# Two cached attention blocks on one core: fewer DMA transposes of P, x loaded in three parts, a shorter warm-up, the output written into its accumulator

## The chip, the cores and the metric

The kernel runs on one core of a Trainium2 chip. The metric is the device time of one execution in microseconds (us), lower is better; the time of a kernel is the median of its runs.

## The reference

Two independent problems, A and B, of the same shape; their results are put side by side along the last axis. All tensors are bfloat16.

```python
# x (16, 80, 576), k_cache and v_cache (16, 16, 512, 128), wq (576, 32*128), wo (32*128, 576)
q = (x @ wq).reshape(B, Sq, Hq, Dh).transpose(0, 2, 1, 3)
k = jnp.repeat(k_cache, 2, axis=1)
v = jnp.repeat(v_cache, 2, axis=1)
scores = jnp.einsum("bhqd,bhkd->bhqk", q, k) * (Dh ** -0.5)
p = softmax(scores, axis=-1)
o = jnp.einsum("bhqk,bhkd->bhqd", p, v)
return o.transpose(0, 2, 1, 3).reshape(B, Sq, Hq * Dh) @ wo
...
return jnp.concatenate([a, b], axis=-1)
```

Each of the 16 heads of K and V serves two query heads, so a K head meets 2 x 80 = 160 query rows.

## The kernel before

**Steps.** The work is cut into 128 steps U, 64 for each problem. A step takes one batch element and four K heads. The 160 query rows of a K head don't fit the 128 rows of a tile, so a step has five score tiles of 128 x 512: one for the first 128 rows of each of the four heads (L678), and one "remainder" tile that collects the last 32 rows of all four (L665).

**What a step does.** TensorE (PE) makes the scores in a PSUM bank. VectorE (DVE) takes the row maximum (L687), ScalarE (ACT) the exponential with its row sum into a slot of `p_sb` (L691), DVE the reciprocal of the sums (L697), GpSimd (POOL) multiplies the slot by it (L700). PE transposes P in blocks of 64 x 64 (L733), and ACT or DVE evict the transposes into `pT` (L751 and L752 for the four main tiles, L757 and L758 for the remainder). PE multiplies `pT` by V (L781), the result goes to `oT` (L795).

**The remainder by DMA.** `rtr` says whether the remainder of a step goes another way: for `RT0 <= U < RT1` and odd U (`RTM`), SyncE (SP) issues a DMA transpose from `p_sb` to `pT` (L740), and PE and the evictions leave the remainder out, so that a step has 32 transposes on PE in place of 40. RT0 is 71 and RT1 is 124 here, which are 27 steps.

**Around the steps.** The projection of q (L542 with a tail of 64 rows in L555, evicted in L568 and L569) runs some steps ahead. The output projection (L827) is done for half of the heads at a time: the first half goes to `acc` in float32 (L839), the second is added and stored (L856 adds, L862 stores). The sum is written to `osb`, which has NOSB = 2 slots, and the store reads it there, so an add waits for the store two before it.

**The start.** GpSimd makes ones and the identity. PE does NWARM matmuls on constants (L353). The first half of x of problem A (five blocks of 128 rows) is loaded in two parts of three and two blocks from SP's queue (L380) into memory that `acc` uses later; GpSimd copies the last 64 columns (L388), PE transposes (L401, L419), DVE evicts (L406, L423). K comes by DMA transpose (L631), V, wq and wo by plain DMA (L635, L507 and L511, L595), all from SP's queue.

**Order.** The order of all instructions on all engines is written out in the string ORDER: each letter takes the next operation of one stream, a mark before it chooses the second engine for an eviction, digits name the PSUM banks. An engine takes its own in that order and waits on semaphores that a pass over the reads and writes works out.

Of the kernel before, what the change touches and what calls it, by code (L numbers as in the profile page):

```python
# [27 lines left out]
NWARM = 8  # L28
# [3 lines left out]
RT0 = 71  # L32
# [19 lines left out]
XLD = ((-100.0, -85.0), (-5.0, -4.9))  # L52
# [11 lines left out]
LETTERS = "abcdefghijklmnopqrstuvwxyzABCDEFGHIJKLMNOPQ"  # L64
ORDER = """
pGMpk7JMJJJJPKl3Gl4JOl5m6OKOKPl3l4Od5KNKd3Kd6ad7d2d1eee'CDd0Dd3CDd5Cd6d7eeDm2d1Dd3CNd6Od2d4Meee'D'CCMd0a'Dd7'D
'Cg1'Ceqg6'Dg2'Cqh5nh7qd3ng0rg1d4nreoqd6C'Dg2d5oqeEnqg4wg7jd3C'DQanqd0wl5Enql6wenOg1wg2Cd5'Dqxng4l3qd0nOqni67O
nEg1Eym3wz'Bqh24w'ADl7ng6xrc0jc'Cqwg1joc5rjwnag2qcoEd6Nwq'ug3'vd4wOnl5qh07nOEri15nwroQg2xd3A'y'Bd0wEq'Cg1oxzi5
6qnwDc7cywnBg4d2'uqg1'Ac7Cc'znm5Ec6qwcH'vg3ENg4'uwHqd7njwDi56naqwh01'zA'yx'Dc3Bng5g7cq'Cc6'vcEqnc4wg2d3rnwcEud
5owqi67'vwrng0Ezb4'AwyD'Bqwog2g7xqg6bnq'Cg0nsd3qnc4g1qcjng2d5Ejqxnai67uwnqh04w'AEyzc1'Crwg6'Bcd3Dnwqg7d5'vqoi1  # L70
2Ernwc0znwcEAc6c'ywu'Bg1g7Cog0xc2qc'Dwg3qc4ncvd5'ujqng1jd6qani27vnEEqxh04'Bzwb3E'yr'AwD'Cg2org7wc6cqnc5wcuod0w
vg1nqd6xqg5nwi24Eqnwg7zbnBwq'Ag1jg5'syd4jqnag2Dd3'Cqni67qnh01EEAnwc5cy'zwr'Bc6g2'ucwEqoc7cwrc5'vcnwg0Dd6Coxg3q
d4'uwvg1nb7qqng0i25HqnHEg3w'ABbj'zyanwqg1'sd5xD'Cqg0nc7cqng2d4unqh36Ei17nrxErob0Eoxg2g3'Aqbw'Bywqng1c7qwd6'z's
Dcnwg0Cd2nwqi34Ewvnjg1zw'yg7'Aqjd5w'Dac3qng0cCd2nBc6'ucqh17vni34ErxEg6E'BAwc0c'z'yd4rwoc3uxocqc1g0w'Ccvng7qc5w
c'uqg3wnb6vwnqjg0d5jqnai17EE'Dwng3Bd2w'Azg0qwg7bDwnqd5'yqni13C'sh04'yz'ABc6'Dcrng1c3qg5ocb7qnCg0'uErjbw'vanqwd
3osxg1g2nqc7d4EEnqwci56wnh01zx'ABg2'Dc5w'yqg6'Cg4cqnb3EEu'vxnd2qjwg7rc5Lwd6qjocwjbnuawng0wi45qrb7'AyozCbEBwg1D
s'swc4cnqg2xc7'vg6qd3nEd4nwEqcg0wui15nxh27ywqb6zwrj'DbnIBj'Ag0Losd4Cc6qcg1'vc3rcng2Eqd5wa'ug0qnwi36nb1B'Aqog2c
3qg6nbq'znyg0g7'Dqcnc2d5ECw'vqc'sd4wni36x'uh01'AyECwg2'z'Bc3Eqcj'Dxg5nc6vLb4wqjjwErbIwoLg7wjcnqd3wnud0rni26Esw
g5y'Bc7xqd4'ACg6'zwncDc2jcqoc3ag0u'vd5qng1cqni27vnEh06EzwB'yg3'Ad1wq'Cd7'Dxrng2i45rwoqwc3'AcEyg0'Bwzc4D'Ccwg5n
# [861 lines left out]
```

## Time and profile before

| | |
|---|---|
| Runs | 718.01, 720.44, 720.60 us; median 720.44 |
| Profiled execution | 720.92 us; its span is 719.0 us |
| Clock of TensorE in the profile | 1.00 |
| PE, DVE, ACT, POOL busy | 712.0, 630.0, 637.5, 431.9 us |
| DMA moved | 164.23 MB, 228 GB/s over the span |

A span is the time from the first to the last instruction of the profiled execution. Rows of the timeline give the start, the length, the engine, the line of the kernel and the operation with its tiles; in brackets stands the idle time before it and what ended it. Matmuls overlap, so the length of one is not its price; the distance from start to start is.

### The profile page before, as it was taken

Reading aid. Unit: us, or ns where it says so; the run is one execution under the profiler, and the core shown is the slowest. Engines: PE = TensorE matmul, PEld = TensorE weight load, DVE = VectorE, ACT = ScalarE, POOL = GpSimd, SP = SyncE. Lnnn points to the kernel's source line nnn. Section 1 sums busy time; section 2 is a strip of 40 time slices with the busy share of each in tenths; the row PEclk is TensorE's granted clock in tenths of the full one; section 3 lists DMA queues with packets and bytes.
Section 4 is the critical chain, followed back from the end, with each engine's and each line's share of the span. In section 5 each row is a group of like instructions: output and inputs, shape, how many; then the busy total and the mean of one; then the engine's idle time right before and its main releaser. Section 6 shows DMA issues by size and latency. Waiting matters only on the chain.

```text
span 719.0 us, 25863 instructions
## 1 busy us (share of the span) xinstructions
PE 712.0 (99%) x10604; PEld 508.8 (71%) x10604; DVE 630.0 (88%) x1419; ACT 637.5 (89%) x1830; POOL 431.9 (60%) x650
## 2 busy tenths in 40 slices
PE   9999999999999999999999999999999999999998
PEld 5576777777777777777777776767677777777777
DVE  3999998899978998899998899878898889998995
ACT  1999998899988998799988999888999898998994
POOL 0467657566655765755774566645676466665783
PEclk9999999999999999999999999999999999999999
DMA  9999999999799998999999999999999999999970
GB/s 238 275 217 240 273 252 250 286 232 244 175 268 241 220 241 194 258 223 240 255 216 248 226 201 206 228 246 239 220 229 204 279 196 261 225 247 221 211 195 18
DMA packets 388853, 164.23 MB, mean 228 GB/s; under 512 B 293248, under 2 KB 385664, under 8 KB 388736
## 3 DMA queue, kind: packets, MB, share of 16 engines
q1 hardware_dynamic: 388736, 162.59, 100.2%
q8 instruction: 84, 1.38, 0.8%
q14 instruction: 33, 0.27, 0.2%
HBM read 87.65 MB, written 2.95 MB: 126 GB/s over the span
## 4 chain that ended last, share of the span: by engine, by line
PE 93%; DMA 2%; DVE 2%; ACT 1%; SPq 0%; issue 0%; ACTq 0%; DVEq 0%
PE ps L827 22%; PE ps L781 20%; PE ps L542 18%; PE ps L678 15%; PE ps L733 10%; PE ps L665 5%; PE ps L555 4%; DVE negmax L687 2%; DMA pT<-p_sb 1%; DMA wq_sb<-in_A_wq_dram 1%; DMA out_dram<-osb 1%; ACT p_sb L691 0%; ACT qT L568 0%; DVE xT L406 0%; DVE qT L569 0%
## 5 line engine op out<-in xcount | busy, mean ns | idle before, releaser
L700 POOL TENSOR_SCALAR p_sb<-p_sb,rinv 128x512 bf16<-128x512 bf16 x640 | 430.1, 692 | 271.4 <-DVE rinv L697 270.8
L691 ACT ACTIVATE p_sb<-ps,negmax 128x512 bf16<-128x512 f32 x640 | 442.7, 713 | 27.3 <-DVE negmax L687 23.5
L687 DVE TENSOR_REDUCE negmax<-ps 128x1 f32<-128x512 f32 x640 | 419.2, 682 | 35.0 <-PE ps L678 30.3
L781 PE MATMUL ps<-pT,v_sb 128*128 128x160 bf16 x2048 | 191.2, 233 | 1.1 <-ACT p_sb L691 0.8
L781 PEld LDWEIGHTS ps<-pT,v_sb 128*128 128x128 bf16 x2048 | 152.8, 98 | 42.6 <-ACT p_sb L691 4.1
L827 PE MATMUL ps<-wo_sb,oT 128*128 128x288 bf16 x1280 | 181.1, 286 | 0.0
L678 PE MATMUL ps<-kT,qT 128*128 128x512 bf16 x512 | 178.0, 380 | 1.2 <-ACT p_sb L691 0.8
L542 PE MATMUL ps<-xT,wq_sb 128*128 128x320 bf16 x1024 | 174.4, 299 | 0.2 <-DMA wq_sb<-in_A_wq_dram 0.2
L827 PEld LDWEIGHTS ps<-wo_sb,oT 128*128 128x128 bf16 x1280 | 122.0, 98 | 42.5 <-ACT p_sb L691 0.8
L691 ACT ACTIVATION_READ_ACCUMULATOR p_sb<-ps,negmax 128x1 f32 x640 | 146.0, 228 | 0.0
L542 PEld LDWEIGHTS ps<-xT,wq_sb 128*128 128x128 bf16 x1024 | 95.4, 98 | 45.0 <-ACT p_sb L691 2.4
L751 ACT COPY pT<-ps 128x512 f32<-128x512 f32 x157 | 92.4, 602 | 13.3 <-PE ps L733 12.8
L733 PEld LDWEIGHTS ps<-ident,p_sb 64*128 64x128 bf16 x4904 | 88.2, 95 | 7.3 <-issue 1.3
L733 PE MATMUL ps<-ident,p_sb 64*128 64x64 bf16 x4904 | 92.4, 190 | 0.3 <-issue 0.2
L752 DVE COPY pT<-ps 128x1024 bf16<-128x1024 bf16 x99 | 67.3, 684 | 11.4 <-PE ps L733 10.0
L568 ACT ACTIVATE qT<-ps 128x320 bf16<-128x320 f32 x133 | 59.0, 458 | 19.3 <-PE ps L555 15.5
L569 DVE TENSOR_SCALAR qT<-ps 128x320 bf16<-128x320 f32 x123 | 58.2, 482 | 10.7 <-PE ps L555 6.1
L795 DVE CAST oT<-ps 128x320 bf16<-128x320 f32 x122 | 58.4, 482 | 7.7 <-PE ps L781 7.4
L678 PEld LDWEIGHTS ps<-kT,qT 128*128 128x128 bf16 x512 | 48.0, 97 | 24.1 <-ACT p_sb L691 4.1
L795 ACT CAST oT<-ps 128x320 bf16<-128x320 f32 x134 | 58.9, 451 | 5.2 <-PE ps L781 4.9
L697 DVE RECIPROCAL rinv<-rowsum 128x3 f32<-128x3 f32 (+1 forms) x256 | 38.4, 160 | 1.8 <-ACT p_sb L691 1.7
L665 PE MATMUL ps<-kT,qT 128*32 128x512 bf16 x512 | 39.2, 384 | 0.0
(31 smaller groups left out, 175.5 us busy)
## 6 DMA issues: line engine op xcount, KB each, us to landing
v_sb<-in_A_v_cache_dram SPq DMA_DIRECT2D x64, 512.0 KB, 5.0
v_sb<-in_B_v_cache_dram SPq DMA_DIRECT2D x64, 512.0 KB, 5.2
wo_sb<-in_A_wo_dram SPq DMA_DIRECT2D x8, 576.0 KB, 5.8
wo_sb<-in_B_wo_dram SPq DMA_DIRECT2D x8, 576.0 KB, 5.8
wq_sb<-in_B_wq_dram SPq DMA_DIRECT2D x4, 1024.0 KB, 6.9
out_dram<-osb SPq DMA_DIRECT2D x40, 72.0 KB, 3.8
wq_sb<-in_A_wq_dram SPq DMA_DIRECT2D x8, 256.0 KB, 4.7
wq_sb<-in_A_wq_dram SPq DMA_DIRECT2D x2, 1024.0 KB, 8.4
```

The lines of the kernel that those rows point to most:

```text
L542: last = e.matmul(ps[:, vbq[h].phys, QO:QO + 320], lhsT=wq_sb[:, wsl, ck, hi * 128:(hi + 1) * 128], rhs=xT[:, half, ck, n0:n0 + 320], star ...
L665: last = e.matmul(ps[32 * g4:32 * g4 + 32, vb_.phys, :], lhsT=qT[:, qsl_, bl_, g4 * 160 + 128:g4 * 160 + 160], rhs=k_of(U_, g4), start=Tru ...
L678: return e.matmul(ps[:, vb.phys, :], lhsT=qT[:, qsl, bl, gl * 160:gl * 160 + 128], rhs=k_of(U, gl), start=True, stop=True)
L687: return e.tensor_reduce(negmax[:, si:si + 1], ps[:, vb.phys, :], axis=AX.X, op=AluOpType.max, negate=True)
L691: return e.activation(p_sb[:, psl, :], ps[:, vb.phys, :], AF.Exp, bias=negmax[:, si:si + 1], scale=1.0, accum_out=rowsum[:, ss, k:k + 1])
L700: return e.tensor_scalar(p_sb[:, psl, :], p_sb[:, psl, :], rinv[:, ss, k:k + 1], 1.0, op0=AluOpType.mult, op1=AluOpType.mult)
L733: last = e.matmul(dst, lhsT=p_sb[64 * h:64 * h + 64, psls[k_], j * 128:(j + 1) * 128], rhs=ident[64 * h:64 * h + 64, 64 * h:64 * h + 64], ...
L751: return e.copy(dst.bitcast(F32), ps[:, vtp[h].phys, :].rearrange("p (j n) -> p j n", j=4))
L752: return e.tensor_copy(dst, psb[:, vtp[h].phys, :].rearrange("p (j n) -> p j n", j=4))
L781: last = e.matmul(ps[:, vo.phys, off:off + 160], lhsT=v_sb[:, vs, gl, j * 128:(j + 1) * 128], rhs=pT[:, pts, j, :, 32 * gl:32 * gl + 32], ...
L795: return (e.copy if en == "act" else e.tensor_copy)(dst, src)
L827: last = e.matmul(ps[:, vb.phys, 0:DC], lhsT=oT[:, sp_ * (HH // 2) + i, rb * 128:(rb + 1) * 128], rhs=wo_sb[:, 2 * c3 + sp_, i, :], start= ...
```

## The change

- RT0 goes from 71 to 97: 14 steps send their remainder by DMA in place of 27. The other 13 transpose it on PE and evict it as the even steps do.
- The first half of x is loaded in three parts, of one, two and two blocks. The first is issued from ACT's queue, the others from SP's. Copies, transposes and evictions of the tail follow these parts.
- NWARM goes from 8 to 5.
- The last add writes its bfloat16 result over the first half of the float32 values that it reads in `acc`, and the store reads it there. `osb` is gone, and with it the wait of an add for an earlier store. An add of problem B into `acc` has the store of problem A from that place to wait for.
- ORDER is another one, with a stream more (the part of x on ACT's queue). On PE the groups of matmuls are partly in another order, and some evictions change between ACT and DVE. On GpSimd the copy of the first block of x stands ahead of the making of the identity.

```diff
-NWARM = 8
+NWARM = 5
...
-RT0 = 71
+RT0 = 97
...
-XLD = ((-100.0, -85.0), (-5.0, -4.9))
+XLD = ((-100.0, -99.9, -85.0), (-5.0, -4.9))
+XENG = (("act", "sp", "sp"), ("sp", "sp"))
...
-        osb = sb("osb", [128, NOSB, DC], BF16)
...
-        XP = ((0, 3), (3, 5))
+        XPS = (((0, 1), (1, 3), (3, 5)), ((0, 3), (3, 5)))
...
-            for part, (k0, k1) in enumerate(XP):
+            for part, (k0, k1) in enumerate(XPS[half]):
...
-                S.add("sp", XLD[half][part], em_ldx,
+                S.add(XENG[half][part], XLD[half][part], em_ldx,
...
-                xk = (XA + 4.0 * part if half == 0 else 5.0 * (16 - LQ) - XH) + 0.1 * part
+                xk = (XA + (0.0, 0.6, 4.0)[part] if half == 0 else 5.0 * (16 - LQ) - XH) + 0.1 * part
...
-                                return e.tensor_tensor(osb[:, slot, :], ps[:, vb.phys, 0:DC],
+                                return e.tensor_tensor(xs[:, rb, 2 * c3 * DC:(2 * c3 + 1) * DC], ps[:, vb.phys, 0:DC],
                                                        acc[:, rb, c3 * DC:(c3 + 1) * DC], AluOpType.add)
...
-                                return e.dma_start(dst, osb[:, slot, :])
+                                return e.dma_start(dst, xs[:, rb, 2 * c3 * DC:(2 * c3 + 1) * DC])
...
-                                  writes=[R(("osb", slot), (prob, half, n))], name="oeb%d.%d.%d" % (prob, half, n),
+                                  writes=[R(("acc", rb, c3), (prob, hh))], name="oeb%d.%d.%d" % (prob, half, n),
...
-                            S.add("sp", xe + 0.3, em_st, reads=[R(("osb", slot), (prob, half, n))],
+                            S.add("sp", xe + 0.3, em_st, reads=[R(("acc", rb, c3), (prob, hh))],
```

More of the change, by code (lines that the diff above doesn't have):

```diff
@@ L62 @@
 WOK = 6.0
-LETTERS = "abcdefghijklmnopqrstuvwxyzABCDEFGHIJKLMNOPQ"
+LETTERS = "abcdefghijklmnopqrstuvwxyzABCDEFGHIJKLMNOPQR"
 ORDER = """
[L66 to L79, printed above, removed]
@@ new lines @@
+g2ni14DEqowc0Ec'zAw'Bc3g7y'Dcwjqg1nc4Hg5wvncjqm2d3xH'COg7qEu'uad6ni24wnqxc1'Azg0ycEnwDh25q'Bwg6Cg7'vc4wrncg1qc
+3ocd0unqd2'vEg4qnwi36rnwb7q'ABog1g3EEg6q'zwbnqx'y'Dg5Cng4wd2sqnwc0d7jqnwcjqi13nxaEunwc6zcAg0'Dwh45'Bq'vg1rd3nE
+d6yoxri07qwoc4Cw'AcEBc5'ywg0'zncqg2wc7'ucDng1qd4'uEg6C'vc0wnqcjd3wq'vag7nxi25Eqnwg0Ad1'yw'z'BEDh26wnqg5b3rx'Cn
+rwc7og4qcc0oucg2vd7nqi06qnjg5zbjE'yq'Awj'CBg0awng4qd1ng6Dd2qni57snqh03'z'BEAwc4ncrc7wg5'ycE'uCc6wog4vcqwd1'uEb
+7rnwqoxg0c6qncwd3D'vg5Eng4wqi26wqHng0HbzxA'Bj'yqnag2g6d5D'sq'Cc4ncqg1d3nuh07qni24ErnxEb6roEoxg1g0qb'Aw'Byqwg2n
@@ new lines @@
+c7qd4w'z'sDcnwg1Cd6qnwi35Evwng0zg2w'y'Aqd7j'Dwjc1qng3acCd6nBc4'ucqh02vni15ErxEg4E'BAwc3c'z'yd5rwoc1uxocqc0g3w'
+Ccvng2qc7wc'uqg1wnb4vwnqg0d3qjni27jEE'Dwang1Bd6w'Azg0qwg7bDwnqd3'yqni12C'sh05'yz'ABc4'Dcrng1c3qg2ocb7qnCg0'uEr
+bw'vnqjwd3oasxg1g2nqc7d4EEnqwci56wnh01zx'ABg2'Dc5w'yqg6'Cg4cqnb3EEu'vxnd2qwg7rc5wd6jqocLwbnujwjng0awi45qrb7'Ay
+ozCbEBwg1Ds'swc4cnqg2xc7'vg6qd3nEd4nwEqcg0wui15nxh27ywqb6zwr'DbnBj'AIg0osd4jCc6Lqcg1'vc3rcng2Eqd5wa'ug0qnwi36n
+b1B'Aqog2c3qg6nbq'znyg0g7'Dqcnc2d5ECw'vqc'sd4wni36x'uh01'AyECwg2'z'Bc3Eqc'Dxg5nc6vb4wqjwELrbjwojg7wcInqd3Lwnud
@@ new lines @@
+0jrni26Eswg5y'Bc7xqd4'ACg6'zwncDc2jcqoc3ag0u'vd5qng1cqni27vnEh06EzwB'yg3'Ad1wq'Cd7'Dxrng2i45rwoqwc3'AcEyg0'Bwz
+c4D'Ccwg5nqc1cqd7nuc2'vcung0d3q'vg1og5Eqxi24nqwb6'ABwnzag0EDg2w'yg4nqbwqnd3Eq'Cxg1nc5qcwg0nd7swEq'uh26nwi45rnw
+rc1'Bjcd0'Ajvg5'zaog1qb4'yDoqc2cng7Euc6wncCg2wd5q'vg1qxni36EEnwbA'Bwq'yg2'zx'sg7qg6nc3wcEqnd4wDd1nuwi25jq'CwjE
+h07ay'BwzAc3ncwrg5'Dg2d6'Cqoc4rd1'vnqci03unEg5w'yb4oqwBng2xbq'z'CAnc7cg6'vg0qc3'Dd5jEqnwg1jcsd7njwqh26ni04r'uE
+Ec1w'Bzd3A'yowg4rcac0wCcoc2qwc'vg5Dng6xb1q'vxung2qd4qg0ni57qnEg6Awb'y'z'DBwng2Eqg5wc7g4sjd0nxqad1'Cwqncc3Eqcni
@@ new lines @@
+26uvh57A'Bd3'yE'zrnxc6cC'Dwg2Eg4orc1wb0qowqng5bwqnjwg2jnd7qwc'si45'uj'vh06'BzEDwg1'ynb5rxqd7wHng2bq'Aoc4Hscc1E
+'uwc'Cg0jd4'vwqng1ri35anqb2oA'y'zg0ng6qb'BEqw'Cc3ng1cwqg7'uc5xcnqd3vnd0Dnsi56h12'Bd4'yr'Ag7'CEg6wjqod5b3qwnMrn
+g1g7zbDEqwi06Esnwqb3owzAnwc1Eg2c'BxMqg0c7'uacwqnd6xb'D'ynwCg1'sg2qc4cd3qnEi05unwh14w'BzEg2'vrwc5'AcHqb7'ywoMHx
+'vg0ng1qbqng2td5'DqF'Cd7nEjri36jnc1Aocc2zg0'BycEqg4x'ujg6'Cc3q'vwcnc5qg1wcnDg2jd0wEq'uad7nwvi34Enqwh56wy'BECd1
+'z'Awrg0nm4wDd3qoxi27Onwc5'Acrwg0'yc4'BzcCog2c7qc'uc1qncg6vd5'uqng0d4Ejqnwai27DnxEvg6'Bg3wyb1q'Awqng0wd7q'Cg2'
@@ new lines @@
+zng6Eqg5wbnDwqng4xd3qni02tnqh16'BEjAwc5'zacnrc2wg0'DycEEg4'uCwc3'vqcoc7wg2qg5nxcqd1nwvd0'uqwi47nrb3EyowC'zg2w'
+Bd6q'Axg1jd7nqg4nbEqanEi25xtnwh13B'D'Ag4wzc0r'yc'Cwg2r'ug5c6owd0qocDd1qni37q'vc4B'zjncc6jug7'AcEyg2w'Dvjd4'CqF
+wnc3g0Fqd6ncqg1ni57EEuwnqh23x'yA'Bc0wc'z'Cg7Dc5'vwarcng0c4wEuog6cqxd5rnd2wqb1owvnqi37h04A'z'Dbr'ynjEwg2'Btg3g6
+oqc7wFcqjb1nEunwg0qbwqnxg2Etg7'Cc3qnwcd5rjnwd6Fai01b2A'B'vq'zg0'Dg1qd3nd6q'ync7Ccnb'uoh01ti57rc4'BFg2c'yIqob7z
+'vE'Dwg0b'CqnxAg6nwg4tg2d3qFb7EjEnEwqLg0qwbnaqwnc4tcwnc6ud5xg0wi47qwErc'Bb2xy'znAwg7bqwvng0g4qd6j'Doc7FEtwcLCc
@@ new lines @@
+5ncEwFqg1d3'ujqwni27vwd4znxDd5'yE'AwCh01M'Bwi36rg2A'zb7'Dqog5y'Bg3rbqoIc6CcnLtc1g0qMncc7aqg2'vd4nEuxcqd5nwg1'u
+c3qnwi06ng7zcq'Dg2g1'Ab5q'vnEywd3Eqng0wEg7qbnxqnd2wEt'Bg1wi05'CqjnxMh46A'ywnFc7zcFrw'Bc0Ld1E'DCwjocrg2wjd3'vqo
+ag5wui04nqwc7'yB'zg6'Acqc2'DcnCg0c3vg4ncqg1d5qqEEu'ung2d6ni03wnqh47w'z'yEB'Ad1wnrc0cwC'Dc3g2'vrxg6ocaqc5wcog0E
+qd4xnqb7wnuwm2ni36Ow'vg0'Bg5zbq'y'AEqnwg2c3t'DjcxEg0nqjg7wh46aq'unc5qcd3nCd2rni01voErxg7'Bb5qw'z'Aywg1nDc4qd0w
+ocg2wnuc7cq'Cg6d4'vqng1Ei37Eqwnjg2w'yzjbnAxq'Dg1'Bwg6Etg4nad3qwd5'Cqwni27qwnEh01Bw'znc6Dcw'Arg7d5'yxq'uc4'CcEo
@@ L133 @@
+3qnxA'Bg2wjh06qnjg1rc7ncqbou'vEc5tnxcc7rwi0234vowg1Bc'Ac5qg6'ucg4ynfg7Eqb3w'vqwng0Fqg1nbjEzwFqnFh26qwnai45rxc7
+'AEg0Bwcob4Etw'urnc7wqg2og5wg3qcb'vqnqc7nctc6ucng0vi1247nqjg6F'zEg5y'Awg2qFb1nFqxjnbqwFnEfBxg0ng6Eti34wqFh57'B
+wEjqc2njg1wcr'Ab4wunEqxc3og0cwqbnw'vni1256wtrFc3w'AcEBg0'zx'uc4c'yqog2wi1356vwqg7'Ac4Bc'ync5zg1qcng6c3vcnEuc5w
+c'ub0Ew'vqqxni3457wnbBw'y'zEAb7wtwc3Fci2456uc1'Ab'B'y'zcc3'vcc4ucb5tvFbb7tFbtF
 """
@@ L381, in em_ldx @@
                                        src.rearrange("(k p) d -> p k d", p=128))
-                S.add("sp", XLD[half][part], em_ldx,
+                S.add(XENG[half][part], XLD[half][part], em_ldx,
                       writes=[R(("xs", half * NRT + k_), 0) for k_ in range(k0, k1)], dsem="d_x%d%d" % (half, part),
-                      name="ldx%d.%d" % (half, part), stream="x")
+                      name="ldx%d.%d" % (half, part), stream="xa" if half == part == 0 else "x")
                 def em_xrp(e, half=half, k0=k0, k1=k1):
```

90 lines of the change are left out of this document (35 added, 55 removed).

## The prediction

> **What bounds the kernel now.** I read the page's first lines, then the busy time by stretches, then the timeline of the start, of the stretch that the new RT0 concerns, and of the end.
>
> ```profile
> span 719.0 us, 25863 instructions
> PE 712.0 (99%) x10604; PEld 508.8 (71%) x10604; DVE 630.0 (88%) x1419; ACT 637.5 (89%) x1830; POOL 431.9 (60%) x650
> ```
>
> ```profile
> 50.00:100.00 50.00, 50.00 (x766) 35.40 (x764) 48.73 (x112) 48.89 (x143) 33.54 (x51) 1.00 1.12 262
> ...
> 413.00:550.00 137.00, 135.33 (x2010) 96.26 (x2009) 120.90 (x267) 124.97 (x360) 86.59 (x129) 1.00 1.04 223
> 550.00:700.00 150.00, 149.64 (x2244) 108.88 (x2236) 134.03 (x297) 135.15 (x384) 95.52 (x144) 1.00 1.04 229
> ```
>
> In the stretches the columns are length, then busy time of PE, PEld, DVE, ACT and POOL, clock, DMA. TensorE (PE) is the bound nearly everywhere: 50.00 of 50 us between 50 and 100, 149.64 of 150 between 550 and 700. Only 413 to 550 us shows a loss, 1.67 us. That is where the odd steps from 71 on send their remainder by DMA; the DMA transposes go on after 550, where PE lacks only 0.36. So there is little idle time to win, and a change is worth the PE work that it adds, less the idle time that it takes away, plus what start and end do. All stretches show clock 1.00, so I take no change of clock later.
>
> **The remainder of P, added work.** RT0 rises from 71 to 97: the odd steps 71 to 95, 13 of them, return to PE. A step on the DMA path has 32 transposes on PE, another 40. The timeline of PE shows both kinds after each other; a group's cost is the distance from its start to the next group's start.
>
> ```profile
> 415.99 0.63 PE L733 MATMUL ps<-ident,p_sb 64*128 64x64 bf16 x32
> 416.55 0.73 PE L781 MATMUL ps<-pT,v_sb 128*128 128x160 bf16 x8
> 417.11 0.38 PE L678 MATMUL ps<-kT,qT 128*128 128x512 bf16 x1
> 417.33 0.71 PE L542 MATMUL ps<-xT,wq_sb 128*128 128x320 bf16 x4
> 417.87 0.44 PE L781 MATMUL ps<-pT,v_sb 128*128 128x160 bf16 x4
> 418.48 0.39 PE L678 MATMUL ps<-kT,qT 128*128 128x512 bf16 x1 [0.17 <-ACT p_sb L691]
> ...
> 419.68 0.38 PE L678 MATMUL ps<-kT,qT 128*128 128x512 bf16 x1
> 420.00 0.31 PE L555 MATMUL ps<-xT,wt 64*128 64x320 bf16 x2
> 420.14 0.75 PE L733 MATMUL ps<-ident,p_sb 64*128 64x64 bf16 x40
> 420.82 0.62 PE L665 MATMUL ps<-kT,qT 128*32 128x512 bf16 x8
> ```
>
> 32 transposes take 416.55 − 415.99 = 0.56 us, 40 take 420.82 − 420.14 = 0.68. Each step that returns costs 0.12 us of PE, 13 steps 1.5 us, all of it on the bound. The order of the changed kernel also goes between whole-array matmuls and tiled ones (L555, L665, L733) 274 times after the first score, before 272. A score costs 0.32 us ahead of a tiled group (419.68 to 420.00) and 0.22 ahead of another (417.11 to 417.33), so a switch costs 0.1 and two cost 0.2 us.
>
> Each returning step also needs two evictions of the remainder:
>
> ```profile
> L757 ACT COPY pT<-ps 128x128 f32<-128x128 f32 x106 | 28.5, 284 | 7.6 <-PE ps L733 7.0
> L758 DVE COPY pT<-ps 128x256 bf16<-128x256 bf16 x96 | 26.1, 283 | 7.3 <-PE ps L733 6.5
> ```
>
> 26 evictions of 0.284 us are 7.4 us on ACT and DVE. From 413 to 550 us ACT has 137 − 124.97 = 12.0 us free and DVE 16.1, which covers them; I take nothing for this. Without that cover they would cost up to 7.4 us (a rival below). SyncE (SP) loses 13 DMA issues and the waits ahead of them, so the loads of K and V behind them can only go out earlier; PE does not wait for those loads in that stretch, so this is worth nothing either.
>
> **The remainder of P, waits that go.** Three places in that stretch hang on a DMA transpose.
>
> ```profile
> 417.64 0.69 ACT L691 ACTIVATE p_sb<-ps,negmax 128x512 bf16<-128x512 f32 x1 [0.40 <-DMA pT<-p_sb]
> ...
> 478.87 1.23 SPq L740 DMA_TRANSPOSE pT<-p_sb  x1
> ...
> 482.33 0.71 PE L542 MATMUL ps<-xT,wq_sb 128*128 128x320 bf16 x4
> ...
> 483.85 0.44 PE L781 MATMUL ps<-pT,v_sb 128*128 128x160 bf16 x4 [0.81 <-ACT p_sb L691]
> ...
> 516.12 0.63 PE L733 MATMUL ps<-ident,p_sb 64*128 64x64 bf16 x32
> 516.38 0.69 ACT L691 ACTIVATE p_sb<-ps,negmax 128x512 bf16<-128x512 f32 x1 [0.64 <-DMA pT<-p_sb]
> 517.21 0.39 PE L678 MATMUL ps<-kT,qT 128*128 128x512 bf16 x1 [0.46 <-ACT p_sb L691]
> ```
>
> The landing of the DMA issued at 478.87, from the view of its line:
>
> ```profile
> DMA to landing us min/median/max: 4.9/4.9/4.9
> ```
>
> At 417.64 and 516.38 an exp has to wait until the DMA has read the remainder whose slot in p_sb it overwrites, and the score on PE waits behind that exp. At 483.85 the product with V waits for the remainder itself: issued at 478.87, landed 4.9 us later, at 483.77 (the row names ACT, which had long been done). Against undisturbed distances PE lost: L781 x4 took 0.61 (417.87 to 418.48) where x8 took 0.56, so 0.33; L542 x4 took 1.52 where 417.33 to 417.87 is 0.54, so 0.98; L733 x32 took 1.09 for 0.56, so 0.53. Together 1.8 us. These steps have no DMA any more, so the waits go; what is late next is PE itself, full in the other stretches. Bounds for this term: all of it (−1.8), or nothing, if the engines behind it are no earlier. I take −1.8, since none of the three names another engine that was working.
>
> **The start.** The rows from the timeline, and the landing of the first load of K (row at 10.01):
>
> ```profile
> 1.24 3.60 PE L353 MATMUL ps<-wo_sb 128*128 128x512 bf16 x8 [1.24 <-DVE wo_sb L346]
> ...
> 4.43 0.34 POOL L388 COPY acc<-acc 128x192 bf16<-128x192 bf16 x1 [3.07 <-DMA acc<-in_A_x_dram]
> ...
> 4.63 1.49 PE L401 MATMUL ps<-ident,acc 128*128 128x128 bf16 x12
> 5.91 0.53 PE L419 MATMUL ps<-ident,acc 128*128 128x128 bf16 x3
> ...
> 6.51 0.61 PE L401 MATMUL ps<-ident,acc 128*128 128x128 bf16 x8
> ...
> 6.96 1.25 PE L542 MATMUL ps<-xT,wq_sb 128*128 128x320 bf16 x8
> ...
> 8.37 2.33 PE L542 MATMUL ps<-xT,wq_sb 128*128 128x320 bf16 x16 [0.16 <-DMA wq_sb<-in_A_wq_dram]
> ...
> 10.01 5.71 SPq L631 DMA_TRANSPOSE kT<-in_A_k_cache_dram  x1
> ...
> 19.45 0.38 PE L678 MATMUL ps<-kT,qT 128*128 128x512 bf16 x1 [0.36 <-ACT qT L568]
> ```
>
> ```profile
> DMA to landing us min/median/max: 9.3/9.3/9.3
> ```
>
> Eight warm matmuls run from 1.24 at 0.43 us each (3.39 us to the x transposes at 4.63), so five end about 2.1 us after 1.24, at 3.4. The first block of x now comes alone, from ACT's queue; the first part, three blocks, landed at 4.43, and I put one block at 3.6 (an estimate, half way between the warm-up's end and 4.43; bounds 3.4 and 4.4). In the changed order the identity is made on GpSimd after its copy of that block. Two GpSimd steps of at most the copy's 0.34 us put the first transpose near 4.3, and the first projection perhaps 0.5 us ahead of 6.96. But the next projection waits for the second piece of wq (8.37), and the first score waits for K: issued at 10.01, landed 9.3 later, at 19.31, after which L678 starts at 19.45 with PE idle for 0.36. SP issues 14 loads ahead of K before and after, with the same bytes on the same DMA engines. So what is won on x ends in a longer wait for K. I take 0; bounds −0.3 (K's issue slides forward because one of the x loads has left SP's queue) to +1.0 (the clock, below). Fewer warm matmuls by themselves remove nothing: they ran beside the load.
>
> **The output in acc.** The eviction no longer waits for the store two earlier. The chain of waits shows one such case, and the end is PE's:
>
> ```profile
> 675.00 3.62 DMA out_dram<-osb
> ```
>
> ```profile
> 712.32 4.08 PE L827 MATMUL ps<-wo_sb,oT 128*128 128x288 bf16 x32
> ```
>
> I take −0.2 for it; bounds 0 and −0.5. The last 32 output matmuls, the eviction and the store after them stand in the same order as before, so the end is worth 0. New is that the first evictions of problem B into acc wait for the stores of A from the same place. Block by block B comes a whole problem later, so this wait is over long before; I take 0.
>
> **Sum.** 1.5 + 0.2 − 1.8 + 0 − 0.2 = −0.3 us. The profiled execution took 720.92 us, 1.9 more than its span; it becomes 720.6. The runs shown have a median of 720.44, 0.5 lower, so the forecast is **720.1 us**, no change.
>
> **Rivals.** A measurement of this kernel tells 0.5% (3.6 us) from no change.
>
> *The idle time only moves.* PE pays the 1.7 us, and the waits of 413 to 550 reappear, since the steps from 97 on still use the DMA and the whole order is new. For it: a new order puts other evictions ahead of an exp. Against: 50 to 100 has steps on PE alone and no idle. 720.44 + 1.7 = 722.1; chance 0.2.
>
> *The clock at the start.* Half speed shows as 12 transposes in 1.28 us (0.107 each, 4.63 to 5.91) and full speed as 8 in 0.45 (6.51 to 6.96). The speed rose 5.3 us after the first matmul, at the latest. With five warm matmuls PE has a gap of about 0.9 us near 3.4 to 4.3; counted from its end, the rise would come at 9.6 instead of 6.5, 3.1 us at half speed, 1.5 us lost, of which the waits at 8.37 and 19.45 (0.16 + 0.36) hide 0.5: +1.0. That gives 721.1; chance 0.15. [...]
>
> *ACT becomes the bound: slower.* The order gives ACT 20 more remainder evictions and 10 more of q, and 7 fewer of oT:
>
> ```profile
> L568 ACT ACTIVATE qT<-ps 128x320 bf16<-128x320 f32 x133 | 59.0, 458 | 19.3 <-PE ps L555 15.5 <-DVE pT L758 1.9 <-PE ps L733 1.3
> L795 ACT CAST oT<-ps 128x320 bf16<-128x320 f32 x134 | 58.9, 451 | 5.2 <-PE ps L781 4.9
> ```
>
> 20 x 0.284 + 10 x 0.458 − 7 x 0.451 = 7.1 us. Each stands ahead of an exp, and the score banks come free by exps. It decides from where ACT has no idle time left; between 50 and 100 us it has 1.1 of 50. In full, with the 1.7 on PE, 720.44 + 7.1 + 1.7 − 1.8 = 727.4, slower by 1.0%. Against it: the average room is 12 us from 413 on. Chance 0.12.
>
> *More comes free than I count.* All idle time of 413 to 550 goes (1.67 us, times 1.84 / 1.44, the three places start to start against their shown idle time: 2.1), K lands 0.3 earlier, osb gives 0.5: 720.44 + 1.7 − 2.1 − 0.8 = 719.2; chance 0.13. That the DMA path is not left at all cannot be: 14 DMA transposes of p_sb remain of 27, and PE has 104 more matmuls.
>
> **Numbers.** Forecast 0.4, the rivals 0.2, 0.15, 0.12 and 0.13. All but the ACT case lie within 0.5%. Beyond the slow edge I put the ACT case and a little of the moved idle time, 0.14; beyond the fast edge 0.05, for a start that gains several us that I see hidden by K; 0.81 between. The range takes in the 719.2 case with 1.6 below it for the spread of the runs (the lowest shown lies 2.4 under the median), and above it the moved idle time, the clock and the milder half of the ACT case: 717.6 to 724.0.
>
> **What would show it.** In the profile after: L733 with 5008 matmuls and 14 transposes of p_sb; PE busy about 1.5 us more between 413 and 550 beside less idle time; no exp waiting for the DMA before step 97; first L678 still near 19.4 with a longer wait ahead of it; full speed by 6.5 to 7 us; DVE's evictions of the output without a wait for stores. Wrong would be: first score well before 19, half speed beyond 8 us, or ACT waits ahead of scores in stretches that were full.

## The result, and the profile after

The changed kernel takes 722.15 us (median of 10 runs, 720.97 to 724.77); the kernel before took 720.21 us beside it (10 runs, 718.01 to 721.15). The ratio is 1.0037, 95% interval [1.0021, 1.0053]: slower by 1.9 us between the medians and by 2.7 us by the ratio, where the prediction had 0.3 us faster. The ratio compares all runs of the two kernels and need not be the quotient of the medians. The profiled execution of the changed kernel took 720.97 us, the shortest of its ten, and that of the kernel before 720.92 us, 0.7 over its median. So the two traces are nearly equally long (spans of 719.0 and 719.2 us). They can show where time is lost, but this pair cannot add up to the 1.9 us.

The page's first lines of the changed kernel:

```profile
span 719.2 us, 26055 instructions
PE 712.2 (99%) x10705; PEld 509.8 (71%) x10705; DVE 629.0 (87%) x1423; ACT 642.4 (89%) x1853; POOL 432.4 (60%) x651
```

Busy time by stretches (length, then PE, PEld, DVE, ACT, POOL, clock, DMA), changed kernel:

```profile
413.00:550.00 137.00, 137.00 (x2139) 99.28 (x2137) 121.91 (x275) 129.61 (x378) 87.17 (x130) 1.00 0.96 222
550.00:700.00 150.00, 149.00 (x2214) 107.69 (x2213) 134.70 (x304) 135.69 (x380) 94.06 (x140) 1.00 0.96 219
```

From 413 to 550 us PE is now busy all the time (135.33 before). From 550 to 700, where RT0 changes nothing, it lacks 1.00 us (0.36 before). The timeline of the start, PE and POOL:

```profile
1.24 2.32 PE L353 MATMUL ps<-wo_sb 128*128 128x512 bf16 x5 [1.24 <-DVE wo_sb L346]
4.50 0.61 PE L401 MATMUL ps<-ident,acc 128*128 128x128 bf16 x4 [0.95 <-POOL ident L340]
...
6.93 1.87 PE L542 MATMUL ps<-xT,wq_sb 128*128 128x320 bf16 x8
8.73 0.31 PE L555 MATMUL ps<-xT,wt 64*128 64x320 bf16 x2
...
19.48 0.31 PE L555 MATMUL ps<-xT,wt 64*128 64x320 bf16 x2
19.72 0.61 PE L678 MATMUL ps<-kT,qT 128*128 128x512 bf16 x2
```

```profile
3.89 0.24 POOL L388 COPY acc<-acc 128x64 bf16<-128x64 bf16 x1 [2.90 <-DMA acc<-in_A_x_dram]
4.15 0.29 POOL L340 TENSOR_SCALAR_AFFINE_SELECT ident<-wo_sb 128x128 bf16<-128x128 bf16 x1
```

PE stands still for 0.95 us after the warm-up, until POOL has made the identity. Then eight projections take 1.80 us (6.93 to 8.73), which at full speed take 1.18 (shown below): half speed lasts, by the starts of the single matmuls, until 8.2 us. The first score begins at 19.72 with no idle time of PE ahead of it. Before, it began at 19.45 after a wait. Of the difference, 0.24 us (19.48 to 19.72) are two matmuls of L555 that the new order puts ahead of the first score and the old one behind it. K is no limit here: its load is issued at 9.39 (10.01 before) and lands 9.3 us later, at 18.7, a full microsecond before the first score.

The place in 550 to 700, from the timeline of PE and SP:

```profile
644.41 0.59 PE L678 MATMUL ps<-kT,qT 128*128 128x512 bf16 x2
646.00 0.99 PE L781 MATMUL ps<-pT,v_sb 128*128 128x160 bf16 x12 [1.00 <-ACT p_sb L691]
```

```profile
630.80 7.15 SPq L631 DMA_TRANSPOSE kT<-in_B_k_cache_dram  x1
637.99 0.59 SPq L862 DMA_DIRECT2D out_dram<-acc  x1
638.63 0.98 SPq L635 DMA_DIRECT2D v_sb<-in_B_v_cache_dram  x2
639.68 1.22 SPq L740 DMA_TRANSPOSE pT<-p_sb  x1
```

The view of L740 for this one issue (step 113):

```profile
DMA to landing us min/median/max: 6.2/6.2/6.2
```

639.68 + 6.2 = 645.9: the product with V starts 0.1 us later. The row names ACT, whose exp and row sum were done by 645.4; the wait is for the DMA. Two scores take 0.43 us from start to start (in the kernel without this wait, below), here 1.59: 1.16 us lost.

### The profile page after: what moved, and what is told of

Read it like the earlier page. It is cut to its first block, busy times and chain, and to the rows that moved or that the text cites. A ratio compares the mean times of both kernels' runs of the same rounds, so it can differ in the third digit from the quotient of the medians.

```text
span 719.2 us, 26055 instructions
## 1 busy us (share of the span) xinstructions
PE 712.2 (99%) x10705; PEld 509.8 (71%) x10705; DVE 629.0 (87%) x1423; ACT 642.4 (89%) x1853; POOL 432.4 (60%) x651
## 4 chain that ended last, share of the span: by engine, by line
PE 96%; ACT 3%; DMA 0%; DVE 0%; issue 0%; POOL 0%
PE ps L827 22%; PE ps L781 20%; PE ps L542 19%; PE ps L678 16%; PE ps L733 10%; PE ps L665 5%; PE ps L555 4%; ACT p_sb L691 2%; DMA acc<-in_A_x_dram 0%; PE ps L401 0%; ACT qT L568 0%; ACT pT L751 0%; DVE negmax L687 0%; ACT oT L795 0%; PE ps L419 0%
## 5 line engine op out<-in xcount | busy, mean ns | idle before, releaser
L691 ACT ACTIVATION_READ_ACCUMULATOR p_sb<-ps,negmax 128x1 f32 x640 | 144.2, 225 | 0.0
L733 PEld LDWEIGHTS ps<-ident,p_sb 64*128 64x128 bf16 x5008 | 89.6, 95 | 7.0 <-ACT p_sb L691 0.7
L733 PE MATMUL ps<-ident,p_sb 64*128 64x64 bf16 x5008 | 93.7, 190 | 0.0
L568 ACT ACTIVATE qT<-ps 128x320 bf16<-128x320 f32 x143 | 63.4, 458 | 17.4 <-PE ps L555 14.5
L795 DVE CAST oT<-ps 128x320 bf16<-128x320 f32 x129 | 61.5, 480 | 6.8 <-PE ps L781 6.2
L569 DVE TENSOR_SCALAR qT<-ps 128x320 bf16<-128x320 f32 x113 | 53.7, 481 | 11.6 <-PE ps L555 7.3
L795 ACT CAST oT<-ps 128x320 bf16<-128x320 f32 x127 | 56.0, 450 | 4.4 <-PE ps L781 4.1
```

The costliest lines, as they stand in the source:

```text
L691: return e.activation(p_sb[:, psl, :], ps[:, vb.phys, :], AF.Exp, bias=negmax[:, si:si + 1], scale=1.0, accum_out=rowsum[:, ss, k:k + 1])
L733: last = e.matmul(dst, lhsT=p_sb[64 * h:64 * h + 64, psls[k_], j * 128:(j + 1) * 128], rhs=ident[64 * h:64 * h + 64, 64 * h:64 * h + 64], ...
L795: return (e.copy if en == "act" else e.tensor_copy)(dst, src)
```

## The experiments

Two theories stood against each other at first. The clock theory: the gap ahead of the transposes keeps TensorE at half speed for some 2 us longer. The work theory: the remainders that return cost more than they give, because the idle time comes back elsewhere. A third came up with the traces: stalls of PE inside one operation, for which the profile names nothing that PE waited for. All times are medians; the ratio, with its interval, is to the kernel before, run beside each.

### The change with eight warm-up matmuls

```diff
-NWARM = 5
+NWARM = 8
```

> The changed kernel with NWARM back at 8 and nothing else. Clock theory (the shorter warm-up leaves a gap on PE, half speed lasts to about 8.2 us in place of 6.4, and the 1 to 2 us lost there are the loss): full speed again by about 6.5 us, first score near 18.8, and the time falls by 0.8 to 1.5 us, to about 720.9. Work theory (13 more steps of transposes on PE cost 1.5 us and the waits that went come back elsewhere): full speed earlier, but the first score waits for K and the time stays within 0.4 us of 722.

721.81 us, ratio 1.0018 [1.0007, 1.0029], where the change has 1.0037 [1.0021, 1.0053]. That is 0.3 us less by the medians and 1.4 by the ratios; the intervals overlap, so the times alone don't decide between the two theories. The start in its timeline of PE does:

```profile
1.24 3.59 PE L353 MATMUL ps<-wo_sb 128*128 128x512 bf16 x8 [1.24 <-DVE wo_sb L346]
4.63 0.63 PE L401 MATMUL ps<-ident,acc 128*128 128x128 bf16 x4
...
6.77 1.25 PE L542 MATMUL ps<-xT,wq_sb 128*128 128x320 bf16 x8
7.95 0.31 PE L555 MATMUL ps<-xT,wt 64*128 64x320 bf16 x2
...
18.97 0.59 PE L678 MATMUL ps<-kT,qT 128*128 128x512 bf16 x2
```

The transposes begin 0.13 us later than in the change and the first score begins 0.75 us earlier. The eight projections take 1.18 us in place of 1.80. So it is the speed and not the moment of the start that was lost. The wait at step 113 is still there:

```profile
646.41 0.99 PE L781 MATMUL ps<-pT,v_sb 128*128 128x160 bf16 x12 [1.30 <-ACT p_sb L691]
```

This trace has two more waits between 550 and 700 that the changed kernel's lacks: 0.63 us at 613.9 and 0.58 at 694.9.

### The kernel before with five, and with eight short ones

```diff
-NWARM = 8
+NWARM = 5
```

> The kernel before with NWARM 5 and nothing else. Clock theory: PE stands idle from 3.4 to 4.6 us, half speed lasts 1.5 to 3 us longer, and the time rises by 0.8 to 1.5 us. Work theory: the longer half speed is hidden by the wait for the second piece of wq and for K, no change (within 0.4 us).

722.19 us, ratio 1.0026 [1.0012, 1.0040]. The gap is there (0.97 us up to 4.52) and half speed lasts until 8.6 us, but the first score, at 19.55, is only 0.1 us later than before. Its profiled execution took 724.4 us, and its waits name another loss:

```profile
PE ps L733 <- issue: 2.7, 2, 1.4
PE ps L781 <- issue: 1.8, 2, 1.6
```

These 4.5 us are stalls in the middle of a group. Three matmuls fewer also give every later instruction of TensorE another number in its count, and the stalls may have to do with that. So the next run keeps the number of instructions and only shortens the matmuls.

```diff
-                last = e.matmul(ps[:, vw.phys, :], lhsT=ones, rhs=warm, ...
+                last = e.matmul(ps[:, vw.phys, 0:320], lhsT=ones, rhs=warm[:, :, 0:160], ...
```

> The kernel before with eight warm-up matmuls of 320 columns in place of eight of 512: the array is busy as long as with five of 512 (2560 columns), and the number of TensorE instructions stays the old one. [...]

721.29 us against 720.57, ratio 1.0016 [0.9995, 1.0036]; half speed until 9.1 us, first score 19.75, stalls of issue 0.3 us in sum.

```profile
1.24 2.31 PE L353 MATMUL ps<-wo_sb 128*128 128x320 bf16 x8 [1.24 <-DVE wo_sb L346]
4.50 1.44 PE L401 MATMUL ps<-ident,acc 128*128 128x128 bf16 x12 [0.94 <-DMA acc<-in_A_x_dram]
```

With the number of instructions kept, half speed is there as with five warm-up matmuls (until 9.1 us, there 8.6), and the stalls of issue are 0.3 us in place of 4.5. The ratio is 1.0016 where it was 1.0026, and its interval reaches 1. The turned-round run has 14 warm-up matmuls of 292 columns (4088 columns in place of 8 x 512 = 4096), so twelve more instructions of TensorE, loads and matmuls, and no gap:

```diff
-NWARM = 8
+NWARM = 14
...
-                last = e.matmul(ps[:, vw.phys, :], lhsT=ones, rhs=warm, ...
+                last = e.matmul(ps[:, vw.phys, 0:292], lhsT=ones, rhs=warm[:, :, 0:146], ...
```

> [...] Clock theory: full speed by 4.6 to 6.6 us and the time of before, 720.4 within 0.6. [...]

721.52 us against 720.57, ratio 1.0008 [0.9993, 1.0022], first score 19.16 (after 0.62 us of waiting for K). Its stalls of issue are 1.5 us in sum, more than the 0.5 of the kernel before. Whether the count of instructions sets the stalls, the run does not settle: the interval takes in no loss as well as 1.5 us. Half speed until 8.2 to 9.1 us in all three kernels with the gap is shown; that it costs 0.7 to 1.8 us is what the medians of the two kernels say in which nothing else was changed, each with an interval of 1 us or more either way.

### The x part alone

```diff
-XLD = ((-100.0, -85.0), (-5.0, -4.9))
+XLD = ((-100.0, -99.9, -85.0), (-5.0, -4.9))
+XENG = (("act", "sp", "sp"), ("sp", "sp"))
```

with the split copies, transposes and evictions, and the old order and identity.

> The kernel before with the x part of the change alone: the first x in three parts, the first of them on ACT's queue, its transposes and evictions split in the same way; eight warm-up matmuls, the identity ahead of the copies on POOL as before, the old order of all else. Theory of the prediction (the x part is worth nothing as long as the warm-up covers the load): first K issue 0.5 us earlier (near 9.5), first score 18.8 to 19.3, time 719.9 to 720.7. Rival, ACT's queue or the extra eviction costs: 721 or more, with ACT's table load later or TensorE waiting between 4.6 and 12 us. Rival, the start gains: 719.3 to 719.9.

721.07 us against 720.87, ratio 0.9997 [0.9979, 1.0014], first score 19.64 after 0.28 us of waiting for K. Three parts on two queues show no gain by themselves behind eight warm-up matmuls: the transposes begin at 4.63 as before, because PE is busy until then. K was issued at 10.13 and not earlier; that and the late first score miss the expectation.

### The output in the accumulator alone

```diff
-        osb = sb("osb", [128, NOSB, DC], BF16)
...
-                                return e.tensor_tensor(osb[:, slot, :], ps[:, vb.phys, 0:DC],
+                                return e.tensor_tensor(xs[:, rb, 2 * c3 * DC:(2 * c3 + 1) * DC], ps[:, vb.phys, 0:DC],
```

> The kernel before with the output written into acc and no osb, in its own order. My forecast: -0.2 us (0 to -0.5), the single wait for a store near 679 us goes. A rival in which the add that reads and writes the same bytes is slower on DVE: its mean goes above 0.45 us, +0.1 to +0.5 us.

721.40 us (7 runs), ratio 1.0010 [0.9992, 1.0029]: no gain that can be seen, though the interval takes in the −0.2 us that were expected. One eviction takes 449 ns as before (450).

### The remainders moved in an order made for something else

The kernel before with 12 of the 13 steps (all but 85) back on PE, their evictions put where the neighbouring steps have theirs:

```diff
-RT0 = 71
+RT0 = 97
...
-            rtr = RT0 <= U < RT1 and (RTM[U % 2] or U >= RT2)
+            rtr = (RT0 <= U < RT1 or U == 85) and (RTM[U % 2] or U >= RT2)
```

> The kernel before in its own order, but 12 of the 13 odd steps from 71 to 95 (all except 85, whose slot is overwritten too early in this order) transpose their remainder on PE and evict it. Work theory: PE gets 12 x 0.12 = 1.4 us more, the waits of 413 to 550 us partly stay: +0.5 to +1.5 us. My forecast and the clock theory: 1.4 us more work, 1.8 us of waits less, -0.4 to +0.2 us.

731.18 us, ratio 1.0162 [1.0146, 1.0178]. PE loses 6.75 us between 413 and 550, much of it in small waits for evictions (PE's busy time in the whole span grows too, from 712.0 to 715.2):

```profile
413.00:550.00 137.00, 130.25 (x1971) 91.24 (x1969) 116.74 (x264) 119.89 (x343) 82.00 (x122) 1.00 0.85 203
```

```profile
PE ps L781 <- ACT pT L757: 1.5, 2, 0.8
PE ps L781 <- DVE pT L758: 1.3, 2, 0.6
```

The other way round, the changed kernel with eight warm-up matmuls and the DMA from step 71 on, each DMA placed after its last condition:

```diff
-RT0 = 97
+RT0 = 71
```

> The changed kernel with eight warm-up matmuls and the DMA remainders from step 71 on again: the thirteen remainders leave TensorE (1.5 to 1.7 us of matmuls) and ACT and DVE (26 evictions), in an order planned with them. Work theory (those matmuls are on the path and the DMA lands in time in this order): 1 to 1.7 us less than the changed kernel with eight warm-up matmuls (721.8), 720.1 to 720.8. Wait theory (each late landing costs more than the 0.13 us of matmuls that it spares): waits of TensorE for the DMA between 413 and 550 us of 1.8 us or more in sum, 721.9 to 723.5.

728.51 us, ratio 1.0105 [1.0081, 1.0129], far from both expectations.

```profile
462.57 0.99 PE L781 MATMUL ps<-pT,v_sb 128*128 128x160 bf16 x12 [0.86 <-DMA pT<-p_sb]
...
501.96 0.72 PE L542 MATMUL ps<-xT,wq_sb 128*128 128x320 bf16 x4 [2.77 <-ACT p_sb L691]
```

The DMA ahead of 501.96 went out at 496.84, behind an issue of K of 9.23 us, and landed 4.3 later, at 501.1. Behind this wait of 2.77 us TensorE's clock fell: the trace has it at half from 503.15 to 506.56, some 1.7 us of work.

```profile
503.00:506.60 3.60, 3.60 (x15) 1.98 (x15) 1.36 (x3) 2.72 (x8) 1.36 (x2) 0.53 1.00 234
```

Neither run prices the RT0 part of the change as it was made, with an order of its own. Both show what such a move costs without one, as I placed the pieces: 10.8 us over the kernel before, and 6.7 us over the changed kernel with eight warm-up matmuls.

The smallest such move, the two steps at which the prediction saw the largest waits, 83 and 89, on PE in the kernel before:

```diff
-            rtr = RT0 <= U < RT1 and (RTM[U % 2] or U >= RT2)
+            rtr = U not in (83, 89) and RT0 <= U < RT1 and (RTM[U % 2] or U >= RT2)
```

> The kernel before with only two steps, 83 and 89, taken off the DMA, those whose late landings cost most in its traces (0.98 to 1.0 us near 482.3 and 0.5 to 1.4 us near 516.1): remainder on TensorE with its evictions, the order else unchanged. Theory of the prediction (a wait for a landing goes for 0.12 us of matmuls): both waits gone, 1.3 to 2.1 us less than before, 718.5 to 719.3. Moved-wait theory (the evictions that come in, in an order not planned for them, give new waits of some 0.7 us a step, as the run with twelve moved steps had it): 720.0 to 721.0, with new TensorE waits of 0.5 to 1 us within 5 us of each place.

721.54 us, ratio 1.0012 [0.9992, 1.0032]. The DMA has left these steps, and the waits have not:

```profile
482.96 0.39 PE L678 MATMUL ps<-kT,qT 128*128 128x512 bf16 x1 [0.41 <-DVE qT L569]
517.54 0.39 PE L678 MATMUL ps<-kT,qT 128*128 128x512 bf16 x1 [0.88 <-ACT p_sb L691]
519.85 0.73 PE L781 MATMUL ps<-pT,v_sb 128*128 128x160 bf16 x8 [0.83 <-ACT pT L757]
```

### Step 113

The changed kernel with eight warm-up matmuls and the remainder of step 113 on PE too:

```diff
-            rtr = RT0 <= U < RT1 and (RTM[U % 2] or U >= RT2)
+            rtr = U != 113 and RT0 <= U < RT1 and (RTM[U % 2] or U >= RT2)
```

> The changed kernel with eight warm-up matmuls and with one more step, 113, taken off the DMA: its remainder goes by TensorE and two evictions, in the place in the order at which its neighbours have theirs. Moved-wait theory (the changed order has a new wait of 1.2 to 1.5 us at step 113, near 646 us): that wait goes, 0.12 us of matmuls come, so 1.0 to 1.3 us less than the changed kernel with eight warm-up matmuls (721.8), 720.5 to 720.8, and no TensorE wait between 640 and 650 us. Rival, idle time only moves on: the wait turns up at the next DMA steps (115 to 123), 721.5 to 722.

721.21 us, ratio 1.0007 [0.9991, 1.0023]; with the step on the DMA it was 1.0018. In place of 1.30 us of idle time there are 0.41, for the eviction that came in:

```profile
644.92 1.00 PE L781 MATMUL ps<-pT,v_sb 128*128 128x160 bf16 x12 [0.41 <-DVE pT L758]
```

That is between the two expectations. Another way is to send the step earlier. The next kernel also cures the start at its other end: the identity is made ahead of the copy of x, so that a shorter warm-up has no longer gap.

```diff
-NWARM = 5
+NWARM = 7
```

In its order the identity stands ahead of the warm-up, as in the kernel before; the first tile of step 113 is normalised three places earlier on POOL, and its DMA stands ahead of one store and two loads of V on SP.

> The changed kernel mended in three places: the identity made ahead of the x copy on POOL (so that seven warm-up matmuls, to about 4.4 us, leave no gap ahead of the transposes), seven warm-up matmuls in place of five, and at step 113 the first part of P normalised three places earlier and its DMA put ahead of two V loads and a store on SP. Clock theory: no gap, full speed by 4.6 to 6.6 us, first score 18.4 to 19.0. Moved-wait theory: the DMA of step 113 issued 1.3 to 1.9 us earlier, so the wait near 646 us falls from 1.2 to 1.5 us to under 0.4. Both: 1.0 to 2.3 us below the changed kernel (722.15), 719.9 to 721.1. If neither cause was the one: 721.5 to 722.5.

720.73 us against 720.87, ratio 0.9988 [0.9973, 1.0004]: the loss is gone. Full speed from 4.7 us, first score 18.85, no wait at 646; this trace has waits of 0.44 us at 614.0 and 0.70 at 693.7 instead. The last run takes NWARM back to 5:

> The mended kernel of the run before (identity ahead of the x copy on POOL, step 113 earlier) with five warm-up matmuls again: the array is free at 3.5 us and the first x is there at about 3.9, so the gap ahead of the transposes is 0.3 to 0.5 us and not the 0.95 us of the changed kernel. If any gap puts the clock off: half speed until 8 us or more, first score 19.3 to 19.8, and 0.7 to 1.5 us more than with seven warm-up matmuls (720.7), 721.4 to 722.2. If it is the length of the gap that counts: full speed by 4.6 to 6.6 us, first score 18.4 to 18.9 and 720.2 to 720.9.

**719.99 us against 721.05, ratio 0.9985 [0.9974, 0.9996]: faster than the kernel before by 1.1 us, the only version here whose interval lies below 1, and that narrowly.** The start and step 113 in its timeline:

```profile
3.93 0.59 PE L401 MATMUL ps<-ident,acc 128*128 128x128 bf16 x4 [0.37 <-DMA acc<-in_A_x_dram]
...
6.42 1.25 PE L542 MATMUL ps<-xT,wq_sb 128*128 128x320 bf16 x8
...
18.91 0.59 PE L678 MATMUL ps<-kT,qT 128*128 128x512 bf16 x2
...
644.75 0.59 PE L678 MATMUL ps<-kT,qT 128*128 128x512 bf16 x2
645.18 0.99 PE L781 MATMUL ps<-pT,v_sb 128*128 128x160 bf16 x12
```

```profile
631.09 7.52 SPq L631 DMA_TRANSPOSE kT<-in_B_k_cache_dram  x1
638.71 1.21 SPq L740 DMA_TRANSPOSE pT<-p_sb  x1
```

```profile
DMA to landing us min/median/max: 2.5/2.5/2.5
```

With a gap of 0.37 us the projections from 6.42 on run at full speed (the clock rises at 5.9 us). The DMA of step 113 goes out 1.0 us earlier and, with no loads of V issued just ahead of it, lands 2.5 us after its issue in place of 6.2: 641.2, four microseconds before it is needed. (In the changed kernel the fourteen DMA transposes land after 2.4 to 6.2 us, and this one is the slowest.) Against the changed kernel the two mends take 0.81 us (first score 19.72 to 18.91) and 1.16 us off the trace, 2.0 in sum; the ratios differ by 0.0052, 3.7 us, with intervals of some 1 us each, which don't overlap. The order of PE, ACT and DVE is the same in both, so it is these two places that made the changed kernel slow. How the loss divides between them is not shown: the eight warm-up matmuls mend one of them alone, and there the intervals overlap. The runs with five and seven warm-up matmuls aren't told apart.

## Why the prediction was wrong

**Two steps failed, the start and the waits that go. The start:** its term was taken as 0, with the clock as its bound of +1.0 and a chance of 0.15. The reason given was that what is won on x ends in a longer wait for K. The trace shows no such wait: K lands at 18.7, and the first score comes straight behind the projections at 19.72, because PE itself was late. In kernels of the old start (eight warm-up matmuls or 14 that take as long, x in two parts) the first score stood between 18.57 and 19.45 us, with x in three parts at 19.64, behind a wait for K; with the gap it stood at 19.55, 19.72 and 19.75. The rival "the clock at the start" was right in kind: half speed lasted to 8.2 us and not to the 9.6 that it worked out, and cost 0.75 us of the trace against the same kernel with eight (0.58 and 0.90 against two others of this start with eight, first scores at 19.14 and 18.82).

The gap itself was seen (0.9 us) and its cause half: the prediction has two POOL steps ahead of the first transpose and puts it at 4.3; it came at 4.50. What it did not weigh is that the identity, needed by every transpose, had been made at 1.06 us in the kernel before (its POOL row) and now waits behind a copy that waits for the load:

```profile
1.06 0.29 POOL L340 TENSOR_SCALAR_AFFINE_SELECT ident<-wo_sb 128x128 bf16<-128x128 bf16 x1
```

That was the part of the new order to be charged for, and putting it back (with five warm-up matmuls kept) takes the gap from 0.95 to 0.37 us.

**The waits that go: right for their stretch, mis-sized for the kernel.** The term was −1.8, more than the idle time that the three rows show (0.17 + 0.81 + 0.46 = 1.44 us). From 413 to 550 the waits did go (PE 137.00 of 137). But one of 1.16 us came at step 113. In idle time the two stretches give −1.0 us (1.67 gone in the one, 0.64 more in the other). Counted over the whole trace behind the first score, waits alone, it is only 0.2: four of 1.66 us in sum before, three of 1.46 us after. This is the rival "the idle time only moves". The run with steps 83 and 89 shows the weak point of the reasoning: a wait that ends with a DMA's landing need not vanish with the DMA, if an eviction or an exp is as late.

Nor is the idle time of an order a fixed price. In its stretch from 413 to 550 the old order left PE busy for 135.33 us in the trace that the prediction read, for 134.85 in the run with the output in acc, and for nearly all of it in the run with 14 warm-up matmuls, which was no faster for that:

```profile
413.00:550.00 137.00, 136.84 (x2041) 97.87 (x2039) 122.25 (x272) 126.88 (x363) 88.27 (x132) 1.00 1.01 228
```

**Work on PE: more, but nearer 1 us than 1.7.** PE's busy time between 413 and 550 grew by 1.67 us, but in a stretch of fixed length that is only the idle time that went. From the first projection to the last matmul, without all the time in which PE stood idle, the kernel before takes 706.1 us and the changed kernel with eight warm-up matmuls 707.1. Three other traces of the old work and an unbroken warm-up (output in acc, 14 warm-up matmuls, x in three parts) give 705.5 to 706.3, the two mended kernels 707.1 and 707.3. L733 has 5008 matmuls and 14 DMA transposes remain, as foretold.

**The output in acc: not told apart.** −0.2 was taken; alone it gives 1.0010 [0.9992, 1.0029], which takes in −0.2 as well as nothing or a loss.

**ACT did not become the bound:** 129.61 of 137 us, and no wait of a score for it in that stretch.

With the work at +1.0, the waits at −0.2 and the clock at +0.75, the prediction's own sum is about +1.5 us, where +1.9 was measured, interval 1.5 to 3.8. These sizes come from single traces, which differ by as much from one execution to the next, so that the sum comes near is partly luck. What the times show is that the two mends together take the loss away (1.0037 to 0.9985). How it splits stays open: the medians don't tell 0.5 us apart, and a single stall of the kind told below is larger.

## What to carry to other kernels

Read the first microseconds for two things apart: when PE begins, and at what speed; behind a shortened warm-up look at the gap to the first real matmul (0.37 us did no harm here, 0.95 did), and a constant that everything needs must not be queued behind a load. When an order is written out by hand or by a planner, a moved piece of work is priced by the order it lands in: twelve of the thirteen remainders cost 10.8 us in the old order, while a kernel with all thirteen in an order made for them was no slower than the kernel before once two places of it were mended. After such a change look for the new wait outside the stretch that was changed, and ask what stands ahead of it on its queue; here a DMA landed after 6.2 us behind two loads of V and after 2.5 without them.

## What the runs showed of the hardware

**The clock.** The traces show it in the distance between the starts of equal matmuls: in the changed kernel transposes of x start 0.107 us apart and the first projections 0.267, and behind 8.2 us it is 0.055 and 0.136. With eight warm-up matmuls of 512 columns full speed was there by 6.51 us (kernel before, eight transposes in 0.45) and by 6.77 (changed kernel with eight, eight projections in 1.18), with seven from 4.7; with a warm-up to 3.5 and 0.37 us of gap (one profile) at 5.9; with such a warm-up and 0.94 to 0.97 us (three profiles) at 8.2, 8.6 and 9.1. What sets these moments is not shown. A wait of that length did not always cost time: with 12 steps back on PE in the old order, PE waited 1.0 us for x, and the first score came at 19.32, 0.13 us ahead of that of the kernel before.

```profile
PE ps L401 <- DMA acc<-in_A_x_dram: 1.0, 1, 1.0
```

A longer wait in the middle was followed by a fall: behind 2.77 us of idle time (the run with the DMA from step 71 on again, shown above) the clock was at half for 3.41 us. That the idle time caused it is not tested. Four of the executions of the kernel before also have a mean clock of 0.998 in place of 1.000, which 3.41 us at half speed in 720, as in that trace, would give; they took 723.41 to 724.55 us, 2.4 to 3.7 over the medians beside them. What set the clock off there is not known, as none of the four is profiled.

**Stalls inside a group of matmuls.** The kernel before, its version with 83 and 89 on PE, and its version with five warm-up matmuls, the same group of 40 transposes in each:

```profile
474.72 0.30 PE L733 MATMUL ps<-ident,p_sb 64*128 64x64 bf16 x9 [0.24 <-issue]
```

```profile
474.75 0.30 PE L733 MATMUL ps<-ident,p_sb 64*128 64x64 bf16 x9 [1.23 <-issue]
```

```profile
477.40 0.26 PE L733 MATMUL ps<-ident,p_sb 64*128 64x64 bf16 x6 [1.29 <-issue]
```

The stall comes ahead of the last nine of the forty, and with three warm-up matmuls fewer ahead of the last six: in these three it goes with the count of TensorE's instructions and not with the work. Counted over weight loads and matmuls it is the same instruction in all three, number 14,041 from 0. Its length differs, 0.24, 1.23 and 1.29 us; the longest single stall in the run with five warm-up matmuls took 1.6 us, as its waits above show. In the kernel before a transfer of the DMA queue named "instruction" begins at 472.26, 2.46 us ahead of the stall; it is one of 84 in the span, by the page:

```profile
q8 instruction: 84, 1.38, 0.8%
```

No run shows that the stalls come from these transfers. The stalls may be a part of the 2 to 8 us by which runs of one kernel differ, as the clock above may be; how large a part is not shown.
